# Natural order of the experts, nine tiles before the first expert's rows, and routing groups of 4, 4, 1, 1, 2

## The chip, the cores and the metric

The kernel runs on one core of one Trainium2 chip. The metric is the device time of one execution in microseconds (us), the median of several. Inside the core five engines run side by side, each through its own instructions strictly in their order: TensorE (PE, with its weight loads, PEld), VectorE (DVE), ScalarE (ACT), GpSimd (POOL) and SyncE (SP, which here only starts DMAs). An instruction whose input is not there holds up everything behind it on its engine.

## The reference

Three stages, float32, 1536 tokens of 512 values (2 sequences of 768, 8 heads of 64):

```python
# 1 attention: 4 sink keys and a causal window of 128
keep = is_sink | in_window
a = softmax(where(keep, scores, -1e9));  x = a @ v            # -> (1536, 512)
# 2 mixture of 8 experts, two per token
noisy = x @ w_gate + log1p(exp(x @ w_noise)) * noise          # (1536, 8)
top2  = the two largest of noisy per token; weights = softmax of the two
for e in range(8):
    h = maximum(x[mask] @ w1[e], 0)                           # 512 -> 1024
    out[mask] += weight * (h @ w2[e])                         # 1024 -> 512
# 3 dense layer, 512 -> 2048 -> 512
h = x @ w_in;  out = (h * tanh(softplus(h))) @ w_out
```

## The kernel before

**Stages.** The tokens go through attention in 12 tiles of 128. For each tile the scores of a head are one matmul (line 98), DVE adds the mask and finds the row minimum (line 100), ACT takes the exponential (line 101), PE turns the result (line 108), DVE and ACT copy it from PSUM (lines 110 and 111), and PE multiplies by v (line 120). One step `s` of the loop is half a tile: four heads. Behind it `finish(s,t)` puts the last steps of a tile on later places of the loop: `fin_c` (sinks, copy of x transposed), `fin_d` (gate matmul), `fin_d2` (turns x back, line 171, and scales it, line 173), `fin_d1` (gate values, lines 161 to 165). `SLOW` and `FAST` say how many thirds of a step later each comes.

**Routing.** Tiles are routed in groups. When the last tile of a group is finished, `route` gives nine steps that are placed after it: `absz` (line 187, DVE), `soft` (189 and 190, ACT), `noisy` (192 to 194), `top` (196, 197), `chosen` (199 to 201; the last writes `sl`, the chosen experts as zeros and ones), `place` (on PE the prefix sums over `sl`, lines 208 to 210; on DVE lines 214 to 216, the last writes `slot`, the row of each token in its expert's area), `rest` (231, 232; the counts `cum`, and the scatters), `weights` (235 to 241) and `count` (244, 245). The tiny DVE instructions handle all tiles of a group at once, so their number hardly grows with the group.

**Scatter and load.** POOL then scatters each tile's x into the DRAM buffer `xg` (line 219), two indirect DMAs per tile, one for each chosen expert. Expert areas are 1536 rows apart. As soon as 16 scatters are issued (8 tiles), SP is given the loads of rows 0 to 255 of the first expert (line 817, `load_x(0,0)` and `load_x(0,1)`); they wait until those scatters have landed. This is sound only if the first expert has 256 rows after eight tiles; `ORDER` puts expert 4 first for that, and `flag` (line 338) compares the count and sends the program into `general`, a slow full computation, where it isn't so. In the same way line 339 looks at expert 7 and lines 340 to 344 at the largest and smallest expert.

**Experts.** The loaded rows are turned on PE (`trans_x`, line 575) and split into a high part `xh` (ACT, line 576) and a low part `xl` (DVE, line 577). Every product is three matmuls (high-high, low-high, high-low). The first expert starts on 256 rows only: `l1(0,f,0,256)` for eight column blocks f, 12 matmuls each (line 593), with ACT line 597 and DVE line 600 behind each, and for the first four of them a weight split (ACT line 553, DVE line 557). The routing of the last group (tiles 10 and 11) runs between these blocks: `rq` is a list from which one entry is taken before and one after each `l1`; `GAPS` says how many empty entries follow each step. After the eight blocks come the second layer `l2(0,0)` and `l2(0,1)` (line 621), and in the middle of `l2(0,1)` the remaining rows of the first expert, 256 to 447, are turned (line 575 again). Their loads wait for all 24 scatters. From then on experts 0 to 7 and the dense layer (lines 713 and 738) follow as almost gapless matmul work.

Two lines matter for what follows:

```python
for k in range(n): V.max(v8[:,k,:],nl[:,k,:])                 # 196, one per tile of the group
for k in range(n): V.max_index(i8[:,k,:],v8[:,k,:],nl[:,k,:]) # 197
```

Of the kernel before, what the change touches and what calls it, by code (L numbers as in the profile page):

```python
# [11 lines left out]
F32=mybir.dt.float32; F32R=mybir.dt.float32r; BF=mybir.dt.bfloat16; I32=mybir.dt.int32; U32=mybir.dt.uint32  # L12
# [1 line left out]
PS=bass.MemoryType.PSUM; DR=bass.MemoryType.DRAM  # L14
U32=mybir.dt.uint32
NEG=-1.0e30
GROUPS=(4,4,2,2)
ROWS7=(128,192)
XB=8
GD=(9,11); LGU=3; ZU=8; LSU=(2,30); WB=(2,4,3)  # L20
# [1 line left out]
WLD=0  # L22
NBS=2
EV=((1,),(1,),(1,),(1,),(1,))+((1,3),)*7
LXB=1; XLU=48; BANKS=(('a',6),('c',2)); BN='aa'; RQ=(1,1); GAPS=(1,0,0,0,3,2,3,0,1)

SLOW=(2,5,6,6); FAST={9:(2,3,4,3),10:(2,4,5,6),11:(2,3,4,3)}; FASTR=(0,0,1,2,2,5,5,6,7); SLOWR=(0,0,1,2,3,5,5,6,7)
EXPERT_STRIDE=1536

ORDER=(4,0,1,2,3,5,6,7)  # L30


def attention(ctx, tc, I, st, C=448, LO=256, dbg=None, W=None):

    nc=tc.nc
# [4 lines left out]
    one=pool('a_one',1); ld=pool('a_ld',2); wk=pool('a_wk',WB[0]); w3=pool('a_w3',WB[1]); end=st['end']  # L40
# [14 lines left out]
    noise=end.tile([128,NT,8],F32,name='noise',bufs=1)  # L55
# [5 lines left out]
    for j in range(3):  # L61
        z=bm[32*j:32*j+32]; nc.gpsimd.memset(z,1.0)
# [8 lines left out]
    QD,V,VS,P,NB,RS,XTP,XTS={}, {}, {}, {}, {}, {}, {}, {}  # L71
# [105 lines left out]
    def route(t0,n,one=one):  # L177
# [39 lines left out]
        def scatter(t,k):  # L217
            nc.gpsimd.memset(spacer,0.0)
            d=nc.gpsimd.indirect_dma_start(out=st['xg'],out_offset=bass.IndirectOffsetOnAxis(ap=st['slot'][:,2*t+k:2*t+k+1],axis=0),in_=st['x',t],in_offset=None)
            for e in scat: tc.declare_no_dep(d.ins,e.ins,reason="rows of other tokens")  # L220

            if len(scat)>=16:
                for e in st['early']: tc.declare_no_dep(d.ins,e.ins,reason="rows of other tokens")
            scat.append(d)
        def rest():
# [31 lines left out]
    def at(h,f): fill.setdefault(h,[]).append(f)  # L257
    def slot(h):
        for f in fill.pop(h,()): f()
    def finish(s,t):  # L260

        o=FAST.get(t,SLOW)
        for k,f in zip(o,(fin_c,fin_d,fin_d2,fin_d1)): at(3*s+k,lambda f=f: f(t))
        if t in groups and t<NT-1:
            for k,f in zip(FASTR if t in FAST else SLOWR,route(*groups[t])):
                if f.__name__!='count' or t in (3,7): at(3*s+o[3]+k,f)
    def place_rows(n):
        for _ in range(min(n,len(scq))): scq.pop(0)()

# [1 line left out]
    for s in range(NS+2):  # L271
        t=s//2
        for u in (2*s,2*s+1):
            if s>=NS: break
            p=u%4
            if p==0 and t+2<NT: load(t+2)
            if u>=ZU and (u-ZU)%2==0 and u<ZU+16: st['zero']((u-ZU)//2,zt)
            if u==WLD: W.load_to(W.ahead)
            if u==3: W.scalars()
            if u==LGU:  # L280
                for j in range(2): nc.vector.tensor_copy(wbd[64*j:64*j+64,:,16*j:16*j+16],wg[64*j:64*j+64])
            if u in LSU: load_sinks(LSU.index(u))
# [12 lines left out]
        place_rows(NBS)
        if len(scat)>=16 and W.xload: W.xload(); W.xload=None
    while scq: place_rows(1)
    assert W.xload is None
    st['route']=route; st['scq']=scq; st['rest']=[fill[h] for h in sorted(fill)]
# [2 lines left out]
def host(inp):  # L302
    q,k,v=inp['q'],inp['k'],inp['v']
    B,H,S,D=q.shape
    qT=q.reshape(B,4,2,6,128,D).transpose(0,3,2,5,1,4).reshape(12,2,D,4,128)
    kt=k.reshape(B,4,2,6,128,D).transpose(0,3,2,5,1,4)
    ks=np.broadcast_to(k.reshape(B,4,2,S,D)[:,:,:,:4].transpose(0,2,4,1,3)[:,None],(B,6,2,D,4,4))
    kT=np.concatenate([ks,kt],-1).reshape(12,2,D,4,132)
    R={}
    for n,z in (('q',qT),('k',kT)):  # L310
        R[n+'P']=np.ascontiguousarray(z).reshape(12,128,4,z.shape[-1])
    vv=np.ascontiguousarray(v.transpose(0,2,1,3)).reshape(1536,512)
    wg=np.ascontiguousarray(np.concatenate([inp['moe_w_gate'][:,ORDER],inp['moe_w_noise'][:,ORDER]],1).reshape(4,128,16).transpose(1,0,2))
    return {**R,'v':vv,'wg':wg,'noise':np.ascontiguousarray(inp['moe_noise'][:,ORDER].reshape(12,128,8).transpose(1,0,2))}


def scalars(tc,I,st):
# [8 lines left out]
def flag(tc,st,C,M=256,LO=256):  # L326

    V=tc.nc.vector; f=st['sf']; n=st['cnt']; w=st['sw']; s=f[:,8:15]; i=w[:,4:5]
    v=f[:,0:2]; lo,hi,g=f[:,2:6:2],f[:,3:6:2],f[:,6:8]
    V.tensor_copy(f[:,2:6],w[:,0:4])  # L330
    V.tensor_scalar(g,lo,0.0,4294967296.0,op0=ALU.is_lt,op1=ALU.mult)
    V.scalar_tensor_tensor(v,hi,4294967296.0,lo,op0=ALU.mult,op1=ALU.add)
    V.tensor_tensor(v,v,g,op=ALU.add)

    V.tensor_scalar(s[:,0:1],f[:,0:1],4.0,None,op0=ALU.not_equal)
    V.tensor_scalar(s[:,1:2],f[:,1:2],128.0,None,op0=ALU.not_equal)

    V.tensor_scalar(s[:,2:3],n[:,7,0:1],float(M),None,op0=ALU.is_lt)
    for j,r in enumerate(ROWS7): V.tensor_scalar(s[:,4+j:5+j],n[:,2*j+1,7:8],float(r),None,op0=ALU.is_gt)
    V.tensor_reduce(s[:,3:4],n[:,11,:],axis=AX.X,op=ALU.max)  # L340
    V.tensor_scalar(s[:,3:4],s[:,3:4],float(C),None,op0=ALU.is_gt)

    V.tensor_reduce(s[:,6:7],n[:,11,:],axis=AX.X,op=ALU.min)
    V.tensor_scalar(s[:,6:7],s[:,6:7],float(LO),None,op0=ALU.is_lt)
    V.tensor_reduce(f[:,15:16],s,axis=AX.X,op=ALU.max)
    V.tensor_copy(i,f[:,15:16])
    st['flag']=i

def general(tc,I,st,W32,out):

    nc=tc.nc; ident=st['ident']; NT=12; E=8
    with ExitStack() as ctx:
# [87 lines left out]
        with ExitStack() as ph:  # L440
            a1=pool('g_c1',1,ph)
            nc.vector.memset(X,0.0)
            for e in range(E):
                w1=a1.tile([128,4,1024],F32,name='gw1'); nc.sync.dma_start(w1,I['w1'][ORDER[e]].rearrange("(k p) f -> p k f",p=128))
                w2=a1.tile([128,8,512],F32,name='gw2'); nc.sync.dma_start(w2,I['w2'][ORDER[e]].rearrange("(k p) f -> p k f",p=128))
                hh=a1.tile([128,8,1536],F32,name='ghh')
                for f in range(8):
                    for g in range(3):
# [40 lines left out]
class Weights:  # L489

    def __init__(s, nc, I, W32):
        s.nc=nc; s.src=[]
        for e in range(8):
            w=I['w1']
            for f in range(2): s.src.append(bass.AP(tensor=w.tensor,offset=w.offset+ORDER[e]*512*1024+f*512,ap=[[1024,128],[128*1024,4],[1,512]]))
            w=I['w2']
            for f in range(2): s.src.append(bass.AP(tensor=w.tensor,offset=w.offset+ORDER[e]*1024*512+f*512*512,ap=[[512,128],[128*512,4],[1,512]]))
        w=W32[0]
        for f in range(4): s.src.append(bass.AP(tensor=w.tensor,offset=w.offset+f*512,ap=[[2048,128],[128*2048,4],[1,512]]))
        w=W32[1]  # L500
# [61 lines left out]
def moe(ctx, tc, I, st, W, out, C=448, dbg=None, W32=None):  # L562
# [285 lines left out]
```

## Time and profile before

| | |
|---|---|
| time, median of 3 runs | 725.09 us (724.52 to 725.22) |
| the profiled execution | 723.85 us, of which its span 722.1 us |
| PE busy | 701.2 us, 97% of the span |
| DVE, ACT, POOL busy | 69%, 52%, 48% |
| granted TensorE clock, mean | 0.997 of full speed |

The profile is of one execution; times inside it are counted from the start of its span. The time around the span is 1.75 us, and the median lies 1.24 us above the profiled execution. The attention fills about the first 109 us. PE's busy time is no measure of its speed there, since its pipelined instructions overlap in the record; waits and the order of events say more.

### The profile page before, as it was taken

To read this page: it belongs to the slowest core of one execution; us is meant where nothing else is said; L and a number is where in the kernel's file an instruction comes from. 1 tells how busy PE (TensorE), PEld (TensorE's weight loads), DVE (VectorE), ACT (ScalarE), POOL (GpSimd) and SP (SyncE) were. 2 spreads that over 40 slices of the span, in tenths; PEclk is the share of its full clock that TensorE was granted. 3 is DMA by queue.
4 is the path that set the end of the run, shared out by engine and by line. 5 is a ranking of instruction groups with operands and counts; after the bars stand their busy time and mean duration, and the time that the engine had idled before them with its cause. 6 is when DMAs were issued, how large, how long until landed. Compare 5 with 4: busy or idle time off the path is not lost.

```text
span 722.1 us, 11302 instructions
## 1 busy us (share of the span) xinstructions
PE 701.2 (97%) x3887; PEld 589.3 (82%) x3887; DVE 501.7 (69%) x1107; ACT 376.6 (52%) x835; POOL 344.4 (48%) x313
## 2 busy tenths in 40 slices
PE   6999899999999999999999999999999999999996
PEld 4776679889898888889898888888888888888884
DVE  4788877689698797979876126799955665454441
ACT  4887763455455454545454445466645544453442
POOL 5336462555364544645454474566774343233221
PEclk9999999999999999999999999999999999999998
DMA  8996364588778678778767356322212010010001
GB/s 264 245 267 205 107 227 149 188 267 278 226 233 255 226 243 277 231 256 247 264 203 224 127 175 185 101 89 73 59 30 85 17 30 1 1 58 1 1 0 63
DMA packets 66448, 111.49 MB, mean 154 GB/s; under 512 B 6672, under 2 KB 21264, under 8 KB 66384
## 3 DMA queue, kind: packets, MB, share of 16 engines
q1 hardware_dynamic: 57520, 90.29, 40.0%
q0 software_dynamic: 3840, 12.59, 5.3%
q10 hardware_dynamic: 5024, 7.83, 3.0%
q8 instruction: 32, 0.52, 0.3%
q14 instruction: 32, 0.26, 0.1%
HBM read 82.36 MB, written 28.31 MB: 153 GB/s over the span
## 4 chain that ended last, share of the span: by engine, by line
PE 86%; DVE 5%; DMA 4%; ACT 2%; issue 1%; POOL 1%; SPq 0%; ACTq 0%; DVEq 0%; POOLq 0%
PE a L593 22%; PE o L738 18%; PE h L713 17%; PE c L621 16%; PE c L618 4%; PE a L98 2%; PE c L120 2%; PE a L575 2%; PE a L108 2%; DMA qp<-in_qP_dram 1%; DMA d<-yd,sloty 1%; ACT p L101 1%; DVE tt L100 1%; DMA xg<-xr,slot 1%; DMA vt<-in_v_dram 1%
## 5 line engine op out<-in xcount | busy, mean ns | idle before, releaser
L557 POOL TENSOR_TENSOR wl<-stg,wh 128x512 fp32r<-128x512 f32 x152 | 200.9, 1331 | 166.7 <-ACT wh L553 158.5
L726 POOL TENSOR_TENSOR u<-u,q 128x512 f32<-128x512 f32 x48 | 77.2, 1609 | 138.3 <-DVE u L721 94.8
L553 ACT ACTIVATE wh<-stg 128x512 fp32r<-128x512 f32 x160 | 99.3, 625 | 37.3 <-DMA stg<-in_w_dram 9.8
L593 PE MATMUL a<-xl,wh 128*128 128x448 f32 (+1 forms) x288 | 100.0, 347 | 0.5 <-DVE xl L577 0.5
L593 PE MATMUL a<-xh,wh 128*128 128x448 f32 (+1 forms) x288 | 100.2, 348 | 0.0
L593 PE MATMUL a<-xh,wl 128*128 128x448 f32 (+1 forms) x288 | 99.9, 347 | 0.0
L718 ACT ACTIVATE u<-h 128x512 f32<-128x512 f32 x47 | 28.1, 597 | 119.5 <-PE h L713 98.2
L719 DVE TENSOR_SCALAR u<-u 128x512 f32<-128x512 f32 x48 | 28.0, 583 | 88.5 <-ACT u L718 88.3
L621 PE MATMUL c<-wh,hh 128*128 128x512 f32 x192 | 77.6, 404 | 0.0
L713 PE MATMUL h<-xh,wh 128*128 128x512 f32 (+1 forms) x200 | 76.2, 381 | 0.0
L713 PE MATMUL h<-xl,wh 128*128 128x512 f32 (+1 forms) x200 | 75.4, 377 | 0.2 <-DVE xl L694 0.2
L713 PE MATMUL h<-xh,wl 128*128 128x512 f32 (+1 forms) x200 | 75.3, 377 | 0.0
L738 PE MATMUL o<-wh,gh 128*128 128x512 f32 x192 | 74.8, 390 | 0.4 <-DVE u L721 0.4
L621 PE MATMUL c<-wh,hl 128*128 128x512 f32 x192 | 75.1, 391 | 0.0
L621 PE MATMUL c<-wl,hh 128*128 128x512 f32 x192 | 74.8, 390 | 0.0
L738 PE MATMUL o<-wh,gl 128*128 128x512 f32 x192 | 74.7, 389 | 0.0
L738 PE MATMUL o<-wl,gh 128*128 128x512 f32 x192 | 74.7, 389 | 0.0
L521 DVE TENSOR_SCALAR dh<-dh 128x256 f32<-128x256 f32 x64 | 46.6, 727 | 27.1 <-ACT dh L519 27.0
L597 ACT ACTIVATE hh<-a 128x448 fp32r<-128x448 f32 (+2 forms) x80 | 36.5, 467 | 50.7 <-PE a L593 49.4
L593 PEld LDWEIGHTS a<-xl,wh 128*128 128x128 f32 x288 | 54.3, 189 | 4.2 <-DVE xl L577 0.7
L101 ACT ACTIVATE p<-tt,nb 128x264 f32<-128x264 f32 (+1 forms) x96 | 46.5, 486 | 21.5 <-DVE nb L100 17.0
L593 PEld LDWEIGHTS a<-xh,wh 128*128 128x128 f32 x288 | 54.3, 189 | 3.6
(186 smaller groups left out, 1448.0 us busy)
## 6 DMA issues: line engine op xcount, KB each, us to landing
stg<-in_w_dram SPq DMA_DIRECT2D x64, 512.0 KB, 4.9
d<-in_w_in_dram SPq DMA_DIRECT2D x32, 256.0 KB, 3.6
d<-in_w_out_dram SPq DMA_DIRECT2D x32, 256.0 KB, 3.7
xr<-xg SPq DMA_DIRECT2D x24, 256.0 KB, 4.6
yd<-ys ACTq DMA_DIRECT2D x23, 256.0 KB, 4.2
wi<-dh SPq DMA_DIRECT2D x32, 128.0 KB, 3.7
wo<-dh SPq DMA_DIRECT2D x32, 128.0 KB, 3.4
stg<-wi SPq DMA_DIRECT2D x8, 512.0 KB, 4.3
```

Source lines behind the costliest of these rows:

```text
L101: nc.scalar.activation(o,tt[:,:n],AF.Exp,bias=NB[t][:,h:h+1],scale=-1.0,accum_out=RS[t][:,h:h+1])
L521: h=T[i][1]; nc.vector.tensor_scalar(h,h,lo,hi,op0=ALU.max,op1=ALU.min)
L553: if hi=='act': s.nc.scalar.activation(h,src,AF.Copy)
L557: (s.nc.gpsimd if lo=='pool' else s.nc.vector).tensor_tensor(s.lo[n][:,j,:],s.stg[n,j//2][:,j%2,:],s.hi[n][:,j,:].bitcast(F32),op=ALU.subt ...
L593: nc.tensor.matmul(p[:,:w],a[:,k,fs],b[:,k,c0:c1],start=(i==0),stop=(i==11)); i+=1
L597: for a,b in seg(c0+skip,c1,t): nc.scalar.activation(high(e,f,a,b),p[:,a-c0:b-c0],AF.Relu)
L618: for i,w in enumerate((wh,wl)): nc.tensor.matmul(p[:2*m],HH[f][:,o:o+2*m],w,start=f+i==0,stop=f==7 and i==1)
L621: for i,(h,w) in enumerate(((high(e,f,o,o+m),wh),(high(e,f,o,o+m),wl),(HL[f][:,d:d+m],wh))): nc.tensor.matmul(p[:m],h,w,start=f+i==0,stop= ...
L713: nc.tensor.matmul(p[:,c],a[:,k,fs],b[:,k,c],start=(i==0),stop=(i==11)); i+=1
L718: nc.scalar.activation(u,p,AF.Exp)
L726: nc.gpsimd.tensor_tensor(u,u,q,op=ALU.mult)
L738: nc.tensor.matmul(O[g][i],a[:,s],w[:,k,:],start=(f==0 and j==0),stop=(f==15 and j==2))
```

## The change

The experts keep their natural order (`ORDER` goes, in the gate weights, the noise, the expert weights and the general path). The first expert is now expert 0, and its 256 rows are asked for when nine tiles (18 scatters) are out; `flag` looks at its count after nine tiles (`n[:,8,0]`). For that tile 8 is routed alone and then tile 9 alone, in place of 8 and 9 together, and tile 8's last steps come earlier (`FAST` has an entry for it). The count for the flag is taken at tile 8 in place of tile 7's. The steps of the last routing stand closer in `rq`.

```diff
-GROUPS=(4,4,2,2)
+GROUPS=(4,4,1,1,2)
-LXB=1; XLU=48; BANKS=(('a',6),('c',2)); BN='aa'; RQ=(1,1); GAPS=(1,0,0,0,3,2,3,0,1)
+LXB=1; XLU=48; BANKS=(('a',6),('c',2)); BN='aa'; RQ=(1,1)
-SLOW=(2,5,6,6); FAST={9:(2,3,4,3),10:(2,4,5,6),11:(2,3,4,3)}; ...
+SLOW=(2,5,6,6); FAST={8:(2,4,5,5),9:(2,3,4,3),10:(2,4,5,6),11:(2,3,4,3)}; ...
-ORDER=(4,0,1,2,3,5,6,7)
...
-            if len(scat)>=16:
+            if len(scat)>=18:
                 for e in st['early']: tc.declare_no_dep(d.ins,e.ins,reason="rows of other tokens")
...
-                if f.__name__!='count' or t in (3,7): at(3*s+o[3]+k,f)
+                if f.__name__!='count' or t in (3,8): at(3*s+o[3]+k,f)
...
-        if len(scat)>=16 and W.xload: W.xload(); W.xload=None
+        if len(scat)>=18 and W.xload: W.xload(); W.xload=None
...
-    V.tensor_scalar(s[:,2:3],n[:,7,0:1],float(M),None,op0=ALU.is_lt)
+    V.tensor_scalar(s[:,2:3],n[:,8,0:1],float(M),None,op0=ALU.is_lt)
...
-    rq=[lambda z=z: [f() for f in z] for z in st['rest']]
-    for f,k in zip(st['route'](12-GROUPS[-1],GROUPS[-1],one=st['const']),GAPS): rq+=[f]+[lambda: None]*k
+    z=[lambda z=z: [f() for f in z] for z in st['rest']]; R=st['route'](12-GROUPS[-1],GROUPS[-1],one=st['const']); nop=lambda: None
+    rq=[z[0],R[0],*z[1:],*R[1:5],nop,*R[5:8],nop,R[8]]
```

The line numbers of the changed file are 2 lower than before's in the parts quoted below. On SP and POOL the order of the instructions is the same as before.

DVE, the routing of tiles 8 and 9 in before, from `absz` to `chosen` (`u`, `nl`, `v`, `i`, `eA`, `s`, `sl` are the routing's small tiles, x is tile 9's):

```order
L187 SCALAR_TENSOR_TENSOR u_1612<-lz 128x16
L111 COPY pts<-a 128x512
L173 TENSOR_TENSOR x<-a,recip 128x512
L192 SCALAR_TENSOR_TENSOR nl_1613<-lz,u_1612 128x16
L193 TENSOR_TENSOR nl_1613<-nl_1613,noise 128x16
L194 TENSOR_TENSOR nl_1613<-nl_1613,lz 128x16
L196 MAX v_1614<-nl_1613 128x8 x2
L197 MAX_INDEX i_1615<-v_1614,nl_1613 128x8 x2
L199 TENSOR_TENSOR eA_1616<-i_1615 128x2 x2
L200 TENSOR_TENSOR s_1617<-iota_156,eA_1616 128x32
L201 TENSOR_TENSOR sl_1618<-s_1617 128x16
L123 TENSOR_SCALAR recip<-rs 128x8
```

The same place in the change: tile 9's routing begins (`u_1629`), and the end of tile 8's stands in between.

```order
L185 SCALAR_TENSOR_TENSOR u_1629<-lz 128x8
L109 COPY pts<-a 128x512
L212 TENSOR_TENSOR s_1451<-s_1451,a 128x16
L213 TENSOR_REDUCE sf_1453<-s_1451 128x2
L214 SCALAR_TENSOR_TENSOR slot<-eA_1450,sf_1453 128x2
L226 TENSOR_TENSOR cum<-cum,sl_1452 128x8
L171 TENSOR_TENSOR x<-a,recip 128x512
L190 SCALAR_TENSOR_TENSOR nl_1630<-lz,u_1629 128x8
L191 TENSOR_TENSOR nl_1630<-nl_1630,noise 128x8
L192 TENSOR_TENSOR nl_1630<-nl_1630,lz 128x8
L233 TENSOR_SCALAR sf_1453<-sf_1453 128x2
L234 SCALAR_TENSOR_TENSOR sloty<-eA_1450,sf_1453 128x2
```

Each row now handles one tile, and all of `absz` to `weights` is there twice; tile 8's first half (`absz` to `chosen`) stands one step of the loop earlier on DVE.

ACT, a step earlier, in before: the copy `sk` of tile 9's sinks (line 129), for which DVE's line 130 waits, comes straight after the two small copies.

```order
L110 ACTIVATE pts<-a 128x512
L138 ACTIVATE sc<-p 128x96
L158 ACTIVATE gs<-a 128x128
L129 ACTIVATE sk<-a 96x128
L101 ACTIVATE p,rs<-tt,nb 128x264 x4
```

In the change:

```order
L108 ACTIVATE pts<-a 128x512
L156 ACTIVATE gs<-a 128x128
L136 ACTIVATE sc<-p 128x96
L187 ACTIVATE u_1446<-u_1446 128x8
L188 ACTIVATE u_1446<-u_1446 128x8
L127 ACTIVATE sk<-a 96x128
L99 ACTIVATE p,rs<-tt,nb 128x264 x4
```

Tile 8's `soft` (two rows) stands ahead of `sk`; and on DVE tile 8's x, gate values and `absz` stand ahead of the instruction that waits for `sk`.

PE, the prefix sums of the last routing among the blocks `l1(0,f)` in before: `wl_745` is a weight tile of blocks 4 to 7, and the sums come between blocks 5 and 6.

```order
L593 MATMUL a<-xh,wl_745 128x256
L208 LDWEIGHTS tri
L208 MATMUL a<-sl_1882,tri 128x8
L210 LDWEIGHTS ones
L210 MATMUL a<-cum,ones 128x8
```

In the change (`wl_467` is a weight tile of blocks 0 to 3):

```order
L591 MATMUL a<-xh,wl_467 128x256
L206 LDWEIGHTS tri
L206 MATMUL a<-sl_1906,tri 128x8
L208 LDWEIGHTS ones
L208 MATMUL a<-cum,ones 128x8
```

The sums moved up by two blocks, to between blocks 3 and 4. On DVE the rows ahead of the last `sl` are the same as before but for one: line 600 of block 3 now stands behind it.

## Rows read from the trace of the kernel before

**Rows 1.** The page, the chain that ended last, shares of the span by engine.

```profile
PE 86%; DVE 5%; DMA 4%; ACT 2%; issue 1%; POOL 1%; SPq 0%; ACTq 0%; DVEq 0%; POOLq 0%
```

**Rows 2.** Stretches: length, busy us of PE, PEld, DVE, ACT, POOL, granted clock, DMA.

```profile
80.00:103.50 23.50, 21.41 (x228) 16.75 (x227) 22.02 (x114) 16.67 (x58) 9.37 (x18) 1.00 0.37 136
103.50:109.00 5.50, 5.50 (x67) 4.82 (x59) 2.65 (x9) 2.43 (x7) 3.19 (x7) 1.00 0.73 281
109.00:132.00 23.00, 20.89 (x143) 18.90 (x143) 14.77 (x62) 7.54 (x18) 6.69 (x9) 1.00 0.42 145
```

**Rows 3.** Waits from 80 to 109 us: us in total, times, longest.

```profile
ACT p L101 <- DVE nb L100: 6.7, 5, 2.2
DVE tt L100 <- PE a L98: 0.4, 1, 0.4
```

**Rows 4.** Timeline of DVE: start, us, operation; routing of tiles 8 and 9.

```profile
95.76 0.17 DVE L187 SCALAR_TENSOR_TENSOR u<-lz 128x16 f32<-128x16 f32 x1
95.86 0.68 DVE L111 COPY pts<-a 128x512 f32<-128x512 f32 x1
...
97.06 0.16 DVE L192 SCALAR_TENSOR_TENSOR nl<-lz,u 128x16 f32<-128x16 f32 x1
...
98.87 0.17 DVE L123 TENSOR_SCALAR recip<-rs 128x8 f32<-128x8 f32 x1
...
101.64 0.17 DVE L214 TENSOR_TENSOR s<-s,a 128x32 f32<-128x32 f32 x1
...
102.84 0.68 DVE L111 COPY pts<-a 128x512 f32<-128x512 f32 x1
```

**Rows 5.** Timeline of DVE and ACT, `absz` with `soft`, and the sinks' copy.

```profile
82.71 0.19 DVE L187 SCALAR_TENSOR_TENSOR u<-lz 128x32 f32<-128x32 f32 x1
...
83.33 0.58 ACT L110 ACTIVATE pts<-a 128x512 f32<-128x512 f32 x1
...
88.58 0.16 DVE L123 TENSOR_SCALAR recip<-rs 128x8 f32<-128x8 f32 x1
88.58 0.27 ACT L129 ACTIVATE sk<-a 96x128 fp32r<-96x128 f32 x1 [0.24 <-PE a L126]
...
88.89 0.29 DVE L130 TENSOR_TENSOR sk<-a,sk 32x128 fp32r<-32x128 f32 x1
```

**Rows 6.** Timeline, scatters 15 and 16, the first two loads, their first use.

```profile
96.24 0.96 POOL L219 DMA_INDIRECT xg<-x,slot  x1 [0.21 <-issue]
...
97.51 0.96 POOL L219 DMA_INDIRECT xg<-x,slot  x1 [0.23 <-issue]
...
100.30 1.10 SPq L817 DMA_DIRECT2D xr<-xg  x2
...
106.93 1.06 PE L575 MATMUL a<-ident,xr 128*128 128x128 f32 x8
```

**Rows 7.** Line 817 over the whole run, from issue to landing.

```profile
DMA to landing us min/median/max: 4.5/5.3/7.1
```

**Rows 8.** Timeline of the last routing, from block 4 to the remaining rows' turning.

```profile
115.81 0.28 PE L593 MATMUL a<-xh,wh 128*128 128x256 f32 x1
117.73 0.17 DVE L201 TENSOR_TENSOR sl<-s 128x16 bf16<-128x16 f32 x1
118.70 0.18 PE L208 MATMUL a<-sl,tri 128*128 128x8 bf16 x1
120.08 0.16 DVE L216 SCALAR_TENSOR_TENSOR slot<-eA,sf 128x4 int32<-128x4 f32 x1
120.52 0.96 POOL L219 DMA_INDIRECT xg<-xr,slot  x1 [13.18 <-DVE slot L216]
128.81 0.89 SPq L817 DMA_DIRECT2D xr<-xg  x2
131.85 1.05 PE L575 MATMUL a<-ident,xr 128*128 128x128 f32 x8 [1.61 <-DMA xr<-xg]
```

More of the change, by code (lines that the diff above doesn't have):

```diff
@@ L24 @@
 EV=((1,),(1,),(1,),(1,),(1,))+((1,3),)*7
-LXB=1; XLU=48; BANKS=(('a',6),('c',2)); BN='aa'; RQ=(1,1); GAPS=(1,0,0,0,3,2,3,0,1)
-SLOW=(2,5,6,6); FAST={9:(2,3,4,3),10:(2,4,5,6),11:(2,3,4,3)}; FASTR=(0,0,1,2,2,5,5,6,7); SLOWR=(0,0,1,2,3,5,5,6,7)
+LXB=1; XLU=48; BANKS=(('a',6),('c',2)); BN='aa'; RQ=(1,1)
+SLOW=(2,5,6,6); FAST={8:(2,4,5,5),9:(2,3,4,3),10:(2,4,5,6),11:(2,3,4,3)}; FASTR=(0,0,1,2,2,5,5,6,7); SLOWR=(0,0,1,2,3,5,5,6,7)
 EXPERT_STRIDE=1536
-ORDER=(4,0,1,2,3,5,6,7)
 def attention(ctx, tc, I, st, C=448, LO=256, dbg=None, W=None):
@@ L312, in host @@
     vv=np.ascontiguousarray(v.transpose(0,2,1,3)).reshape(1536,512)
-    wg=np.ascontiguousarray(np.concatenate([inp['moe_w_gate'][:,ORDER],inp['moe_w_noise'][:,ORDER]],1).reshape(4,128,16).transpose(1,0,2))
-    return {**R,'v':vv,'wg':wg,'noise':np.ascontiguousarray(inp['moe_noise'][:,ORDER].reshape(12,128,8).transpose(1,0,2))}
+    wg=np.ascontiguousarray(np.concatenate([inp['moe_w_gate'],inp['moe_w_noise']],1).reshape(4,128,16).transpose(1,0,2))
+    return {**R,'v':vv,'wg':wg,'noise':np.ascontiguousarray(inp['moe_noise'].reshape(12,128,8).transpose(1,0,2))}
 def scalars(tc,I,st):
@@ L443, in general @@
             for e in range(E):
-                w1=a1.tile([128,4,1024],F32,name='gw1'); nc.sync.dma_start(w1,I['w1'][ORDER[e]].rearrange("(k p) f -> p k f",p=128))
-                w2=a1.tile([128,8,512],F32,name='gw2'); nc.sync.dma_start(w2,I['w2'][ORDER[e]].rearrange("(k p) f -> p k f",p=128))
+                w1=a1.tile([128,4,1024],F32,name='gw1'); nc.sync.dma_start(w1,I['w1'][e].rearrange("(k p) f -> p k f",p=128))
+                w2=a1.tile([128,8,512],F32,name='gw2'); nc.sync.dma_start(w2,I['w2'][e].rearrange("(k p) f -> p k f",p=128))
                 hh=a1.tile([128,8,1536],F32,name='ghh')
@@ L494, in __init__ @@
             w=I['w1']
-            for f in range(2): s.src.append(bass.AP(tensor=w.tensor,offset=w.offset+ORDER[e]*512*1024+f*512,ap=[[1024,128],[128*1024,4],[1,512]]))
+            for f in range(2): s.src.append(bass.AP(tensor=w.tensor,offset=w.offset+e*512*1024+f*512,ap=[[1024,128],[128*1024,4],[1,512]]))
             w=I['w2']
-            for f in range(2): s.src.append(bass.AP(tensor=w.tensor,offset=w.offset+ORDER[e]*1024*512+f*512*512,ap=[[512,128],[128*512,4],[1,512]]))
+            for f in range(2): s.src.append(bass.AP(tensor=w.tensor,offset=w.offset+e*1024*512+f*512*512,ap=[[512,128],[128*512,4],[1,512]]))
         w=W32[0]
```

## The prediction, made before the changed kernel ran

> **What bounds the kernel now.** I read the chain that ended last, then the stretches between 80 and 132 us, then the waits and the timeline there, because the change moves instructions only there. The chain is 86% PE [rows 1], and behind 132 us that means matmuls without gaps. The chain alone doesn't say what sets the end of the attention. The stretches do: from 80 to 103.5 us DVE is busy 22.02 of 23.5 us, PE 21.41, but PE's times overlap in the record [rows 2]. Who waits for whom decides: ACT waited 6.7 us in five waits for DVE's row minima (line 100), while DVE waited for PE's scores once, 0.4 us [rows 3]. So up to 103.5 us DVE is the clock, and what is added to it ahead of the last scores comes out at the end of the attention. From 103.5 to 109 us DVE is busy 2.65 of 5.5 us; there PE works off the last tiles, in order. From 109 us on PE is the clock, with one wait that matters: at 131.85 us it has waited 1.61 us for the remaining rows of the first expert [rows 8].
>
> **The second routing on DVE.** In before tiles 8 and 9 cost DVE one set of small instructions: 0.10 us for `absz` (95.76 to 95.86), 1.81 for `noisy` to `chosen` (97.06 to 98.87), 1.20 for `place` to `weights` (101.64 to 102.84), together 3.11 us for 23 instructions [rows 4] (a `max_index` is two). A group of one tile has 19: one MAX, two of the index, and one of `rest` fall away. By their number that is 3.11 x 19/23 = 2.57 us; if only the instruction of `rest` saves anything, 3.11 x 22/23 = 2.97. I take 2.8, between the two, because most of these instructions need the one ahead and so don't get closer in a smaller group. The first half, `absz` to `chosen`, is 1.91 us for 14 instructions; with 11 it is 1.50 to 1.91, and I take 1.75. Ahead of the last four score instructions DVE had one first half (1.91); now it has all of tile 8 (2.8) and the first half of tile 9 (1.75). That is 2.64 us more, between 2.57 + 1.50 - 1.91 = 2.16 and 2.97. The rest of tile 9 comes behind the last scores, where before had more. Tile 8's x and gate values are moved, not added.
>
> [...]
>
> **A wait of DVE for the sinks.** Tile 8's `absz` now stands on DVE directly ahead of tile 9's `recip` (line 123) and `sk` (line 130), and on ACT `soft` stands ahead of the copy for which line 130 waits. From `absz` to the end of `soft` are 0.62 us (82.71 to 83.33) and from the copy to line 130 another 0.31 (88.58 to 88.89) [rows 5]: 0.93 us, in which DVE has work for 0.10 + 0.17. That is an idle 0.66, of which before has 0.31 - 0.17 = 0.14. So +0.5; nothing, if DVE comes there late for other reasons. Queued behind it are the next four score instructions, for which ACT waits. In return DVE's one wait for scores, 0.4 us [rows 3], goes, since DVE is now later than PE there.
>
> **End of the attention:** 2.6 + 0.5 - 0.4 = 2.7 us later, bounds 2.16 - 0.4 = 1.8 and 2.97 + 0.5 = 3.5. PE comes to the turning of the first expert's rows at 106.93 + 2.7 = 109.6 us.
>
> **The first rows, after 18 scatters.** In before the sixteenth was issued at 97.51, SP's loads started 2.79 us later, at 100.30, and PE used them at 106.93 without a wait [rows 6]. Now DVE comes to the copy that stood at 95.86 [rows 4] by 1.75 + 0.5 - 0.4 later, at 97.7; with the copy (0.7) and two small instructions (0.4) tile 8's `slot` begins at 98.8, and the scatter 0.44 after it (120.08 to 120.52, [rows 8]) at 99.2, when POOL is just free of the sixteenth. Scatters follow each other by 1.27 us (96.24 to 97.51), so the eighteenth goes at 100.5, has landed at 103.3, and the loads land 5.3 us later, at 108.6 and half of 1.10 after that [rows 6, 7]. PE comes at 109.6 and needs the second half a turning later, at 110.1. I cost it at nothing; the attention's own 2.7 us hide it. Should a load take the 7.1 us of the slowest, the second is there at 110.95 and PE waits 0.8. What stands behind these loads on SP (a stage of weights, line 545) starts 3 us later; the four weight splits of the blocks that follow use stages loaded before.
>
> **The last routing.** The sums (line 208) now stand two blocks earlier on PE: it asks for `sl` when block 3 is done, in before's times at 115.81, where before asked at 118.70. But in before `sl` began on DVE only at 117.73 and was there at 117.9 [rows 8]. Ahead of it DVE has the same instructions as before but one, line 600 of block 3, and ACT's `soft` now delays one weight split by about as much; I keep 117.9, give or take 0.4. So PE waits 117.9 - 115.8 = 2.1 us, and blocks 4 to 7 and the second layer stand behind it. It reaches the remaining rows 2.1 us later than its 131.85 - 1.61 = 130.24, at 132.3. They are there at 131.85 or earlier, so the 1.61 us go, and 0.5 is lost (all of this 2.7 later). Were there no wait for `sl`, this part would give 1.6 back; with 2.5 us it costs 0.9.
>
> **The rest costs nothing.** The order of the experts changes only addresses. The count for the flag is one small copy (line 245) and one sum in either. SP and POOL have the same order.
>
> **Sum:** 2.7 + 0.5 = 3.2 us. The profiled execution of 723.85 us would be 727.05; the median lies 1.24 above it, so **728.3 us**. Its own bounds: 1.8 + 0.1 (`sl` 0.4 earlier) and 3.5 + 0.9, that is 727.0 to 729.5. The runs of before spread over 0.7 us; 0.2%, 1.45 us, is about what a measurement can tell from no change.
>
> **Rivals.**
> - *No wait for `sl`* (0.14): ACT and DVE catch up, `sl` is there when block 3 ends, and the 1.61 us come back: 2.7 - 1.6 = +1.1, 726.2 us. It takes DVE 2.1 us earlier than in before; DVE was busy only 14.77 of 23 us there [rows 2], but the instructions ahead of `sl` are tied to the blocks' ends.
> - *The rows come late* (0.10): DMA slower than [rows 7], or `slot` later; each us beyond the 0.5 of cover counts in full. With 0.8 to 1.5: 729 to 730.
> - *Cheap small instructions* (0.06): they follow each other by 0.10 as `absz` and its neighbour do [rows 4]; 30 x 0.10 - 1.91 = 1.1 in place of 2.6, so 1.7 in all, 726.8 us. The mean of 3.11/23 = 0.135 speaks against it. [...]
> - *DVE has room* (0.07), the other sign: its idle 1.5 us before 103.5 and 2.85 after it [rows 2] take up all that is added, neither the last scores nor `sl` come late, and the 1.61 us are gained: 725.1 - 1.6 = 723.5 us. It decides for "faster" only if what DVE costs, both places together, stays under 0.16 us. ACT's 6.7 us of waiting for DVE speak against it.
> [...]
> - *The change doesn't do what it says* (0.01): with fewer than 256 rows for expert 0 after nine tiles the general path would run as well, far outside any range given here. Counted from the reference with its seed 0 there are 287 (252 after eight).
>
> **How the numbers follow.** My forecast has 0.60. The range goes from just under the first rival to the late rows, 726.0 to 730.0; it holds forecast, first three rivals, without their tails. Faster: the fourth rival, 0.07. Same (up to 726.54): the first rival and a little of the third, 0.16. Slower: 0.77.
>
> **What would show it.** Right: between 86 and 104 us DVE still without gaps but for one before line 130; the last four score instructions some 2.7 us later; no wait at the first turning; a wait of about 2 us at line 208 (206 in the changed file) in the blocks, and none at the second turning. Wrong: DVE waiting for PE's scores more than once, a wait of PE for `xr` at the first turning, or `sl` ahead of PE.

## The result and the profile after

| | before | changed |
|---|---|---|
| median of 10 runs | 723.29 us (722.00 to 725.24) | 727.46 us (726.21 to 730.25) |
| ratio | | 1.0058 [1.0043, 1.0073] |
| profiled execution, its span | 723.85, 722.1 | 728.75, 726.6 |
| mean granted clock of that execution | 0.997 | 0.990 |

The changed kernel is 4.2 us slower. These runs and those of the first four experiments met a kernel before of 723.2 to 723.3 us ("the first chips" below), the eight kernels after them ran on two other chips where it takes 737.8 and 739.3 us, so each kernel is compared only with runs of before on its own chip.

The chain that ended last, shares by engine, to be held against [rows 1]: PE as before, DVE and ACT one more each, DMA one less.

```profile
PE 86%; DVE 6%; DMA 3%; ACT 3%; issue 1%; POOL 1%; SPq 0%; ACTq 0%; DVEq 0%; POOLq 0%
```

Waits between 80 and 111 us (in total, times, longest), to be held against [rows 3]:

```profile
ACT p L99 <- DVE nb L98: 8.1, 5, 2.9
PE a L106 <- DVE sk L128: 1.8, 2, 1.3
DVE sk L128 <- ACT sk L127: 0.6, 1, 0.6
```

ACT waits more for DVE's row minima (8.1 in place of 6.7 us). DVE no longer waits for scores, and has the new wait of 0.6 for the sinks' copy. In no term of the prediction: PE waits for DVE's `sk`, 1.3 us at the longest, where before had 0.2.

DVE's timeline, to be held against [rows 4, 5]: the sinks' wait, tile 8's `slot`, tile 9's `absz` and `sl`, the last four score instructions.

```profile
90.56 0.29 DVE L128 TENSOR_TENSOR sk<-a,sk 32x128 fp32r<-32x128 f32 x1 [0.60 <-ACT sk L127]
...
97.26 0.22 DVE L185 SCALAR_TENSOR_TENSOR u<-lz 128x8 f32<-128x8 f32 x1
...
98.40 0.16 DVE L214 SCALAR_TENSOR_TENSOR slot<-eA,sf 128x2 int32<-128x2 f32 x1
...
100.99 0.17 DVE L199 TENSOR_TENSOR sl<-s 128x8 bf16<-128x8 f32 x1
...
101.82 0.43 DVE L98 CUSTOM_DVE_ANT_0 tt<-a,m 128x264 f32<-128x264 f32 x1
```

PE's timeline, to be held against [rows 6, 8]: PE's wait for `sk`, the first turning, the sums of the last routing, the second turning.

```profile
101.61 1.93 PE L106 MATMUL a<-ident,p 128*128 128x128 f32 x8 [1.35 <-DVE sk L128]
103.47 1.88 PE L118 MATMUL c<-pts,vt 128*64 128x128 f32 x16
...
110.52 1.06 PE L573 MATMUL a<-ident,xr 128*128 128x128 f32 x8
...
121.25 0.18 PE L206 MATMUL a<-sl,tri 128*128 128x8 bf16 x1 [1.70 <-DVE sl L199]
...
137.03 0.99 PE L573 MATMUL a<-ident,xr 128*128 128x128 f32 x8
```

Both turnings come without a wait. The wait for `sl` is where the prediction put it. But behind both waits PE is slow: line 118's 16 matmuls take 1.88 us, where the same 16 of before (line 120) took 1.09:

```profile
99.99 1.09 PE L120 MATMUL c<-pts,vt 128*64 128x128 f32 x16
```

The stretches (columns as in [rows 2]; the granted clock stands third from the right) say why:

```profile
88.40:101.60 13.20, 10.44 (x93) 7.86 (x92) 11.79 (x65) 6.99 (x26) 10.47 (x20) 1.00 0.47 180
101.60:105.30 3.70, 3.69 (x25) 3.10 (x26) 2.36 (x11) 2.58 (x9) 0.00 (x0) 0.54 0.60 181
105.30:110.50 5.20, 5.20 (x66) 4.32 (x65) 3.21 (x14) 1.81 (x5) 2.10 (x4) 1.00 0.69 227
110.50:121.20 10.70, 8.55 (x70) 8.11 (x69) 7.53 (x28) 5.51 (x13) 0.00 (x0) 1.00 0.13 27
121.20:126.00 4.80, 4.75 (x31) 4.71 (x32) 2.65 (x12) 0.38 (x1) 2.64 (x5) 0.64 0.76 281
```

Right behind each of PE's two new waits the mean granted clock was 0.54 and 0.64; in steps of 0.1 us it stood at 0.50 from 101.7 to 105.1 us, where most of line 118's 16 matmuls lie, and from 122.2 to 125.5. In the other three stretches the mean was 1.00. In before it was at 1.00 there throughout [rows 2].

The first rows' way went as forecast: tile 8's second scatter and the loads' issue (line 817 of before), to be held against [rows 6]:

```profile
100.09 0.96 POOL L217 DMA_INDIRECT xg<-x,slot  x1 [0.23 <-issue]
...
102.84 1.10 SPq L816 DMA_DIRECT2D xr<-xg  x2
```

### The profile page after: what moved, and what is told of

It reads as the page before. It is cut to its first block, busy times and chain, and to the rows that moved or that the text cites. A ratio compares the mean times of both kernels' runs of the same rounds, so it can differ in the third digit from the quotient of the medians.

```text
span 726.6 us, 11322 instructions
## 1 busy us (share of the span) xinstructions
PE 703.8 (97%) x3886; PEld 591.6 (81%) x3886; DVE 503.4 (69%) x1122; ACT 376.1 (52%) x837; POOL 343.9 (47%) x313
## 4 chain that ended last, share of the span: by engine, by line
PE 86%; DVE 6%; DMA 3%; ACT 3%; issue 1%; POOL 1%; SPq 0%; ACTq 0%; DVEq 0%; POOLq 0%
PE a L591 22%; PE o L737 18%; PE h L712 17%; PE c L619 17%; PE c L616 4%; PE c L118 2%; PE a L573 2%; PE a L96 2%; PE a L106 2%; DMA qp<-in_qP_dram 1%; ACT p L99 1%; DVE tt L98 1%; DMA stg<-wi 1%; DMA vt<-in_v_dram 1%; PE xt L690 0%
## 5 line engine op out<-in xcount | busy, mean ns | idle before, releaser
L519 DVE TENSOR_SCALAR dh<-dh 128x256 f32<-128x256 f32 x64 | 48.9, 763 | 27.2 <-ACT dh L517 27.2
L99 ACT ACTIVATE p<-tt,nb 128x264 f32<-128x264 f32 (+1 forms) x96 | 46.5, 486 | 22.5 <-DVE nb L98 18.4
```

What stands on the lines that cost most here:

```text
L99: nc.scalar.activation(o,tt[:,:n],AF.Exp,bias=NB[t][:,h:h+1],scale=-1.0,accum_out=RS[t][:,h:h+1])
L519: h=T[i][1]; nc.vector.tensor_scalar(h,h,lo,hi,op0=ALU.max,op1=ALU.min)
```

## The experiments

**Theory:** the attention ends some 2.4 us later because of the second routing on DVE; in the last routing a wait for `sl` takes the place of the one at the second turning, at about the same price; and PE's new waits let the clock fall, which costs more. **Rivals:** the low clock is an accident of one execution; or the last routing's order is the main cost.

A common zero is needed, since all starts differ by up to 1 us: DVE's sum of the counts of tiles 4 to 7 (`cum<-cum,cw`, 88.49 in before, 88.27 in after). Times behind it, read from the timelines of PE and DVE on the first chips (the last of the four score instructions starts 1.06 us behind the first, at 12.19 and 14.61):

| us behind the zero | before | changed, 1st | changed, 2nd | old order | spare matmuls | split on POOL |
|---|---|---|---|---|---|---|
| first of the last four score instructions | 11.13 | 13.55 | 13.54 | 13.54 | 13.54 | 13.55 |
| first turning | 18.44 | 22.25 | 20.90 | 20.90 | 21.18 | 20.91 |
| second turning | 43.36 | 48.76 | 45.91 | 45.55 | 47.00 | 48.32 |
| from first to second | 24.92 | 26.51 | 25.01 | 24.65 | 25.82 | 27.41 |

The new order of the experts, which no run changes by itself, costs nothing behind the table: from the second turning to the end of the span are 590.25 us in before (722.1 less 131.85) and 589.57 in the changed kernel (726.6 less 137.03).

**1. The changed kernel once more**, no edit.

> The changed kernel once more, beside the others on one chip. Theory (what its trace showed): against before the last scores on DVE come 2.2 us later because of the second routing; PE waits 1.35 us for DVE's sinks (line 128) and 1.70 us for sl (line 206), and after each of the two waits the granted clock is at half for some 3.5 us, which costs about 1.4 and 1.5 us; the 1.61 us wait at the second turning is gone. So again 4 us over before, and both stretches at the low clock in the trace. Rival: the low clock is an accident of that one profile; then one or both stretches are at 1.00 here and the time is 2 to 3 us over before.

Measured: 727.87 us, 1.0061 [1.0046, 1.0077]. Both waits stand in its profile (1.35 and 1.69 us), yet the stretches behind them are at full clock:

```profile
101.10:105.00 3.90, 3.85 (x42) 3.11 (x46) 3.59 (x20) 3.07 (x10) 0.55 (x1) 1.00 0.54 168
...
119.30:126.00 6.70, 6.67 (x57) 6.54 (x58) 3.33 (x15) 1.53 (x5) 4.09 (x7) 1.00 0.85 312
```

So the waits stand in both executions, the clock's fall in one of them. The table prices it: without it 2.46 us more than before at the first turning and 2.55 at the second; with it 3.81 and 5.40, so the two low stretches cost about 1.35 and 1.5.

This execution lost 1.2 us elsewhere. Behind the fourth turning of rows PE waits for the last low half of the next expert's rows:

```profile
161.53 0.47 PE L591 MATMUL a<-xl,wh 128*128 128x448 f32 x1 [1.19 <-DVE xl L575]
```

The same wait, 0.9 to 1.3 us, stands in six of the 14 profiles of this study, one of them of before itself (below). It isn't tied to the change; an execution has it or not.

**2. The waits filled:** 9 spare matmuls ahead of the wait for `sk`, 12 ahead of the sums.

```diff
             ps=misc()
+            if t0==10:
+                for _ in range(12): nc.tensor.matmul(ps[:,128:256],ident,ident,start=True,stop=True)
...
             c=misc(); nc.tensor.matmul(c[:,0:8],ones,cum,start=True,stop=True)
+            if t0==8:
+                for _ in range(9): nc.tensor.matmul(c[:,128:256],ident,ident,start=True,stop=True)
```

> The changed kernel with spare matmuls (identity by identity, into unused columns of PSUM tiles that PE holds anyway) queued just before its two waits: 9 behind the count at tile 8, 12 ahead of the last routing's sums. They add work that lies in the waits. Theory (waiting PE loses its clock, and that costs 2.9 us): the granted clock stays at 1.00 from 100 to 130 us, PE reaches the second turning about 2.9 us earlier than in the changed kernel, and the time is 1.3 to 2 us over before. Rival (the clock falls for another reason, or the low clock hides in waits that would come anyway): same time as the changed kernel, or slower by the 2.9 us that the spare matmuls take.

Measured: 728.49 us, 1.0066 [1.0052, 1.0079]: 5.3 us above before, not the 1.3 to 2 expected. The matmuls took longer than the waits (2.25 and 2.84 us), which costs 1.1 up to the second turning by the table. No stretch from 88 to 135 us is below 1.00:

```profile
101.70:105.30 3.60, 3.60 (x42) 3.26 (x41) 3.01 (x17) 2.71 (x10) 0.00 (x0) 1.00 0.51 146
...
121.20:126.00 4.80, 4.80 (x46) 4.75 (x45) 2.15 (x13) 0.77 (x2) 3.15 (x6) 1.00 0.78 266
```

Its five runs spread over 1.5 us (727.91 to 729.37) and have mean clocks of 0.996 to 0.999, where the changed kernel's first ten spread over 4.0 at 0.990 to 0.999. That alone proves little: the changed kernel's six runs of experiment 1, on the same chip, have mean clocks of 0.995 to 0.999 too and spread over 3.2 us, and its profile had no fall either. Less the 1.1 the median would be 727.4, an estimate: by it the clock costs the changed kernel's median on this chip (727.87) about half a microsecond, not three, and that is within the spread of the runs.

**3. The old order of the last routing** in the changed kernel.

```diff
-    rq=[z[0],R[0],*z[1:],*R[1:5],nop,*R[5:8],nop,R[8]]
+    rq=[*z]
+    for f,k in zip(R,(1,0,0,0,3,2,3,0,1)): rq+=[f]+[nop]*k
```

> The changed kernel with the last routing's steps as far apart as in before (its sums between blocks 5 and 6). Theory: no wait of PE for sl, no low clock behind it (1.85 + 1.5 us less), and the wait of 1.6 us at the second turning is back: 1.7 us faster than the changed kernel, 2.4 over before. Rival (following closely pays, the wait for the rows is worth more): slower than the changed kernel by up to 1.6 us.

Measured: 727.0 us, 1.0048 [1.0031, 1.0064]. No wait for `sl`; the wait at the second turning is back:

```profile
PE a L573 <- DMA xr<-xg: 1.7, 2, 1.3
```

Against experiment 1 it gains 0.36 us up to the second turning, and 0.9 in the medians, whose intervals overlap; expected were 1.7, with the cost of the clock counted in. So most of the loss, 3.8 of 4.7 us on this chip, comes with groups and experts' order, and little with the last routing's order.

**4. `sl` sooner?** DVE's four weight splits in the blocks go to POOL, to take 0.68 us each out of DVE's way to `sl`.

```diff
-        if W.k<16: W.split(lo='dve')
+        if W.k<16: W.split(lo='pool')
```

> The changed kernel with the low halves of the four weight splits among the blocks on POOL in place of DVE (line 555, 0.6 us of DVE each; POOL is idle there). Theory: sl comes about 1.8 to 2.4 us earlier, when block 3 ends; PE doesn't wait for it (less than 0.4 us), the clock behind it stays at 1.00, and the 1.61 us at the second turning stay away: 3 us faster than the changed kernel, 0.5 to 1.5 over before. Rival (sl is tied to the blocks' ends by ACT and line 598, not to DVE's load): the wait stays over 1.3 us and the time is that of the changed kernel.

Measured: 727.99 us, 1.0064 [1.0043, 1.0086], and `sl` came later; PE waited 2.6 in place of 1.7. DVE's and then POOL's timeline:

```profile
117.49 1.15 DVE L197 TENSOR_TENSOR eA<-i 128x2 f32<-128x2 uint32 x2
118.68 1.18 DVE L198 TENSOR_TENSOR s<-iota,eA 128x32 f32<-128x32 f32 x1
119.89 0.17 DVE L199 TENSOR_TENSOR sl<-s 128x16 bf16<-128x16 f32 x1
...
116.03 3.78 POOL L555 TENSOR_TENSOR wl<-stg,wh 128x512 fp32r<-128x512 f32 x3 [0.92 <-ACT wh L551]
```

The first two rows (the first is two instructions) take 1.15 and 1.18 us in place of the 0.23 and 0.19 of experiment 1, and end about when POOL's second and third of the three splits do; MAX and the index beside them kept their times (0.23 and 0.16 us). Why these two took longer and those not is not shown.

In its profile the clock did fall behind the wait for `sl`; that is 1.5 of the 2.4 us by which the turnings lie further apart than in experiment 1 (27.41 against 25.01), and the longer wait is 0.9:

```profile
120.00:124.50 4.50, 4.38 (x28) 4.38 (x29) 2.03 (x12) 0.38 (x1) 2.74 (x5) 0.62 0.98 348
```

**The later eight kernels** met something that the first chips don't show. The kernel before, profiled there with no edit:

> The kernel before, profiled once more. The profiled execution of the changed kernel's second run lost 1.2 us at about 160 us, where PE waited for DVE's low half of the next expert's rows, and two of the four changed kernels show this wait, but neither the first profile of before nor the first of after. If this wait is a matter of chance in every kernel, the times of before in the second profile agree with the first up to the second turning (last scores 12.2 us, first turning 18.4, second turning 43.4 us behind the sum of tiles 4 to 7 on DVE, each within 0.3), and the wait may stand here too. If it comes from the change, it is absent here. No low clock between 90 and 140 us by the theory that the two new waits of PE are what lets it fall; if it falls here too, the clock has nothing to do with the change.

It took 739.21 us (one run; median of before there 737.81). Its timelines of ACT, DVE and POOL:

```profile
99.99 0.60 ACT L147 ACTIVATE xts<-c 128x512 f32<-128x512 f32 x1 [6.58 <-remote]
...
117.18 0.27 ACT L129 ACTIVATE sk<-a 96x128 fp32r<-96x128 f32 x1 [4.27 <-remote]
...
100.14 0.43 DVE L100 CUSTOM_DVE_ANT_0 tt<-a,m 128x264 f32<-128x264 f32 x1 [6.98 <-remote]
...
97.35 0.96 POOL L219 DMA_INDIRECT xg<-x,slot  x1 [0.22 <-issue]
...
115.17 0.96 POOL L219 DMA_INDIRECT xg<-x,slot  x1 [0.21 <-issue]
```

ACT and DVE stand twice, for nothing that the profile can name ("remote"), PE with them. They go on 2.6 us behind tile 7's last scatter (97.35) and 2.0 behind tile 9's (115.17); the eight scatters between 80 and 100 us in before on the first chip landed 2.8 us after their issue (median). In before on the first chip ACT's line 147 stood at 92.87 with a wait of 0.36. So the agreement within 0.3 us that was expected is missed: the first turning comes 30.5 us behind the zero, not 18.4. Behind each stand the clock is near 0.5 (stretches):

```profile
100.00:104.00 4.00, 3.36 (x16) 3.36 (x17) 2.84 (x12) 3.12 (x11) 0.00 (x0) 0.50 0.55 187
...
112.00:116.00 4.00, 3.25 (x46) 2.47 (x46) 0.40 (x1) 0.92 (x3) 3.34 (x7) 1.00 0.49 188
116.00:120.00 4.00, 1.71 (x15) 1.68 (x16) 1.93 (x6) 1.27 (x4) 0.21 (x2) 1.00 0.19 74
120.00:124.00 4.00, 4.00 (x19) 3.70 (x19) 1.86 (x4) 0.57 (x2) 0.00 (x0) 0.52 0.02 6
```

The low clock is thus there without the change too, but again behind places where PE stood. And the 1.2 us wait of experiment 1 is there too, in before:

```profile
PE a L593 <- DVE xl L577: 1.3, 1, 1.3
```

**5. Only the last routing's new order**, in the kernel before; run on both chips.

```diff
-    rq=[lambda z=z: [f() for f in z] for z in st['rest']]
-    for f,k in zip(st['route'](12-GROUPS[-1],GROUPS[-1],one=st['const']),GAPS): rq+=[f]+[lambda: None]*k
+    z=[lambda z=z: [f() for f in z] for z in st['rest']]; R=st['route'](12-GROUPS[-1],GROUPS[-1],one=st['const']); nop=lambda: None
+    rq=[z[0],R[0],*z[1:],*R[1:5],nop,*R[5:8],nop,R[8]]
```

> The kernel before with the last routing's steps of the changed kernel, and nothing else. By the reasons as the runs so far leave them: PE waits 1.7 to 2.1 us for sl in the blocks and no longer at the second turning, which comes 0.1 to 0.5 us later than before; 0 to +0.5 us, 723.2 to 723.7, and up to 1.5 more in executions in which the clock falls after the wait. By the rival that this order gives back the second turning's 1.61 us because sl is early when DVE has no second routing ahead of it: 1.6 less, 721.6. By the rival that this order carries most of the change's 4 us: 726 or more.

> The kernel before with the last routing's steps of the changed kernel, once more: in the first run of it the kernel before itself took 737.8 us, because ACT, DVE and PE stood for 4 to 7 us twice between 93 and 117 us, waiting for nothing that the profile names. Without these stands the two explanations are as before: PE waits 1.7 to 2.1 us for sl in the blocks and not at the second turning, 0 to +0.5 us against before, up to 1.5 more where the clock falls; or sl is early and 1.6 us are gained; or the order carries most of the 4 us. Where the stands are there again, they move sl and the rows alike and the difference is again within 1.5 us.

Measured: 0.9984 [0.9965, 1.0003] and 0.9988 [0.9968, 1.0009]. PE waits 1.7 us for `sl` and not at the second turning (waits of the second run):

```profile
PE c L145 <- DVE sk L130: 3.2, 1, 3.2
PE a L208 <- DVE sl L201: 1.7, 1, 1.7
```

That this order carries most of the 4 us is out. Between no difference and a gain of 1.6 us the intervals don't decide; the wait for `sl` is there also without a second routing ahead of it.

**6. Spare matmuls of the right number**, 5 and 7, in the changed kernel; run on both chips.

```diff
+                for _ in range(7): nc.tensor.matmul(ps[:,128:256],ident,ident,start=True,stop=True)
...
+                for _ in range(5): nc.tensor.matmul(c[:,128:256],ident,ident,start=True,stop=True)
```

> The changed kernel with 5 spare matmuls of ident by ident behind the count of tile 8 and 7 ahead of the last routing's sums, by the 0.24 us each that the longer lists of the earlier run took: 1.25 and 1.66 us, as long as the waits that they stand in. They fill PE's waits and add nothing behind them. If the half clock after the waits is caused by PE standing idle, no stretch between 96 and 139 us is below 1.00 and the runs lie 1.5 to 2 us below those with 9 and 12 spare matmuls, that is at 726.5 to 727, at or up to 1 us below the changed kernel, with less spread than its 3 us. If the clock falls whatever PE does, low stretches are there too, and the median is the changed kernel's or above.

> The changed kernel with 5 and 7 spare matmuls in PE's two new waits, once more, for the same reason. By the theory that PE's standing idle lets the clock fall: no stretch below 1.00 between 96 and 139 us, 2.9 to 3.7 us above before, where the changed kernel was 4.2 to 4.6 above it. By the theory that the clock falls whatever PE does: low stretches there, and 4 us or more above before. With the stands of the other run present, below before, as there (1.8 us).

Measured: 0.9976 [0.9955, 0.9998] and 0.9926 [0.9900, 0.9951]: on these chips *faster* than before, by 1.8 and 5.5 us. The first expectation had been written for the first chip and fails by the sign. The first stand is there, with a clock of 0.50 behind it, the second isn't: the four scatters of tiles 8 and 9 now go in two pairs that start 7.3 us apart, and ACT and DVE have no "remote" wait behind 102 us. Behind 108 us the clock is 1.00, as the theory of PE's standing idle has it. The same stretches as above, of the second run:

```profile
112.00:116.00 4.00, 4.00 (x50) 3.26 (x50) 1.68 (x9) 1.81 (x5) 2.10 (x4) 1.00 0.85 295
116.00:120.00 4.00, 3.56 (x37) 3.08 (x33) 2.85 (x8) 1.85 (x4) 0.00 (x0) 1.00 0.24 92
120.00:124.00 4.00, 3.59 (x30) 3.59 (x31) 2.42 (x7) 1.01 (x3) 0.00 (x0) 1.00 0.00 0
```

How the changed kernel fares there without spare matmuls was not run.

**7. Tiles 8 and 9 as one group**, natural order and 18 scatters kept; run on both chips.

```diff
-GROUPS=(4,4,1,1,2)
+GROUPS=(4,4,2,2)
...
-                if f.__name__!='count' or t in (3,8): at(3*s+o[3]+k,f)
+                if f.__name__!='count' or t in (3,9): at(3*s+o[3]+k,f)
...
-    V.tensor_scalar(s[:,2:3],n[:,8,0:1],float(M),None,op0=ALU.is_lt)
+    V.tensor_scalar(s[:,2:3],n[:,9,0:1],float(M),None,op0=ALU.is_lt)
```

> The changed kernel with tiles 8 and 9 routed as one group again (4,4,2,2), still with the rows of the first expert asked for after 18 scatters. DVE has one first half ahead of the last scores as in before, so these should come 12.2 to 12.8 us behind the sum of tiles 4 to 7, 2 us earlier than in the changed kernel, if its second routing on DVE is the cost that I put it down to; 14.6 as in the changed kernel, if that cost lies elsewhere (order of the experts, the count). The 17th and 18th scatter go at about 102.5 and 103.8 us, the loads 2.8 later and land 5.3 behind, at about 112, so PE waits 4 to 5 us at the first turning, and 1.7 for sl in the blocks: the second turning some 5 us later than before, 728 to 728.5, no better than the changed kernel, and worse by 1 to 3 if the clock falls after these waits. By the rival that the loads have several us of room, no wait at the first turning and 725 to 726.

> The changed kernel with tiles 8 and 9 routed as one group, once more, since in its first run the kernel before took 737.8 us. Last scores 12.2 to 12.8 us behind the sum of tiles 4 to 7 if the second routing on DVE is the cost, 14.6 if not. Loads of the first rows land at about 112 us: PE waits 4 to 5 us at the first turning and 1.7 for sl, 4.5 to 5.5 us above before, and 1 to 3 more where the clock falls. By the rival that the loads have several us of room, 1 to 2 us above before.

Measured: 1.0019 [0.9999, 1.0040] and 1.0020 [0.9993, 1.0047]. The question of DVE's cost got no answer: the stand fixes when DVE goes on, and the first of the last four scores starts 18.6 us behind the zero (20.0 in before there). The rows kept PE 0.6 and 0.9 us, not 4 to 5: the second stand is back with four scatters in a row, and in it PE waited 3.2 and 2.4 us ahead of the turning. The waits of the second run:

```profile
PE c L143 <- DVE sk L128: 2.4, 1, 2.4
PE a L206 <- DVE sl L199: 1.7, 1, 1.7
PE a L573 <- DMA xr<-xg: 0.9, 1, 0.9
```

**8. The sums one block earlier than in before**, one later than in the changed kernel.

```diff
-GAPS=(1,0,0,0,3,2,3,0,1)
+GAPS=(1,0,0,0,1,2,3,0,1)
```

> The kernel before with the last routing's sums one block earlier than it has them, one block later than in the changed kernel. By the arithmetic of the prediction: PE asks for sl at 117.25 (block 4's end), DVE has it at 117.9, so 0.65 us of wait; slot and the rows come 0.8 earlier than in before, 131.05, PE comes at 130.24 + 0.65 = 130.89: 0.16 of wait is left of 1.61. In all 0.8 us less than before, a ratio of 0.9989. If sl follows PE's blocks (DVE later whenever PE asks earlier), the wait for sl is 1.2 or more and nothing is gained. If the rows' way after the sums is longer than in before, the second turning still waits 0.5 or more.

Measured: 0.9963 [0.9939, 0.9987]. The waits are what the arithmetic gives, 0.5 us for `sl` (0.65 forecast) and none at the second turning:

```profile
PE c L145 <- DVE xr L173: 1.5, 1, 1.5
PE a L208 <- DVE sl L201: 0.5, 1, 0.5
```

The gain of 2.7 us by the ratio is more than the 0.8 foretold, whose ratio of 0.9989 lies just outside the interval. What made the rest isn't shown; in its profile the second stand is shorter as well, and the instructions up to there are those of before. Against the profile of before on the other late chip the first turning, ahead of which the edit changes nothing, is already 1.6 us early (28.84 against 30.46 us behind the zero), and the second 2.2. It beats before on that chip; on the first chips it wasn't run.

**The clock over all 14 profiles.** Seven have a wait of 1.7 us or more for `sl` ahead of the last routing's sums: both of the changed kernel, the splits on POOL, and experiments 5 and 7 on both chips. In six of them the clock is 0.50 from 2 to 4 us behind the start of the sums; only experiment 1 stays at 1.00. In the other seven PE doesn't wait there, waits 0.5 us, or the wait is filled, and the clock is 1.00 in all. Experiments 5, 7 and 8 in their second or only runs:

```profile
136.00:140.00 4.00, 4.00 (x26) 3.91 (x25) 1.39 (x9) 0.38 (x1) 3.26 (x7) 0.69 0.97 369
...
132.00:136.00 4.00, 4.00 (x27) 3.95 (x27) 1.55 (x9) 0.77 (x2) 3.34 (x7) 0.73 0.96 328
...
132.00:136.00 4.00, 4.00 (x30) 3.71 (x30) 1.97 (x10) 1.01 (x4) 3.35 (x7) 1.00 0.93 348
```

Experiment 5 puts the wait into the kernel before, experiments 2, 3 and 6 take it out of the changed kernel, and the fall comes and goes with it. So the wait for `sl` lets the clock fall to 0.50, in six of the seven profiles that have it. Behind the wait for `sk` it fell in one of the four profiles of the first chips that have this wait unfilled.

## Why the prediction was right, and where it was not

The forecast rested on four terms and a base. The terms can be checked one by one in the traces; no run that changes only DVE's second routing gave an answer (experiment 7), so its cost is read from the rows, not isolated.

**DVE's second routing** (2.64 forecast, bounds 2.16 to 2.97): right in kind, 0.3 too large. In after's timeline tile 8's set is 2.61 us (0.11 + 0.47 + 1.06 + 0.55 + 0.42, five pieces between other work; 2.8 forecast) and tile 9's first half 1.64 (1.75 forecast). Less 1.91 that is 2.34. The small instructions follow each other as in before, about 0.14 us apart, so the rival of cheap small instructions is out.

**The sinks' wait** (0.66 forecast): 0.60. **DVE's wait for scores** (0.4): gone. In sum 2.34 + 0.46 - 0.36 = 2.44, and the last scores came 2.42 later (13.55 against 11.13). That DVE has room is refuted with it.

**The first rows** (hidden): right. `slot` at 98.40 (98.8 forecast), the loads' issue at 102.84 (103.3), no wait at the first turning. The prediction's list of rivals speaks of 0.5 us of cover; its own times leave 1.0 (109.6 against 108.6).

**The last routing** (a wait of 2.1 for `sl`, 0.5 lost): the wait is 1.7, so 1.70 - 1.61 = 0.1 is lost; 25.01 against 24.92 us between the turnings in the execution without low clock.

**What was not in the sum.** PE's wait of 1.35 us for `sk`. It alone delays nothing: at full clock the first turning is 2.46 later, as the last scores are. But it is one of the two waits behind which the clock fell to 0.50. **The granted clock** is in no term of the sum either. Behind the wait for `sl` it falls in six of seven profiles. The price is 1.5 us there, since it lasts about 3.4 us, and 1.35 more where it falls behind the wait for `sk` as well. In another execution of the same kernel it stayed at 1.00 behind both (experiment 1), so a chance that is an on-or-off for the kernel is the wrong form for it.

**0.4 us lie outside the span**, which the prediction left at before's value without a word. The time around the span is 1.71 us in before and 2.13 in the changed kernel (medians over their runs). It is 2.1 to 2.2 in each kernel with five groups but the one with splits on POOL (1.75). Why isn't settled.

**The sum.** 2.5 to 2.6 us in the span at full clock and 0.4 around it are 3.0, near the 3.2 forecast. Measured are 4.2 and 4.7. How the remaining 1.2 to 1.7 divide between the clock and chance waits like that of 1.2 us stays open. For the clock speak the 1.5 us behind the wait for `sl` in most profiles, and the first ten runs: the four with a mean clock of at most 0.992 have a median of 729.4 us, the other six 726.9. Against it speak the six runs of experiment 1, all at 0.995 or more and yet at 727.87, and the half microsecond of experiment 2. A pair of profiles can't settle it, since single executions lie up to 3 us apart: the one of before was 0.6 us above its median of ten, the one of experiment 1 the fastest of its six, 1.1 below their median. The forecast of 728.3 lies only 0.8 above the measured median because a second miss goes the other way, and that is luck: its base, the median of three runs of before (725.09), was 1.8 above that of ten.

## What to carry to other kernels

A new wait can cost more than its length: the wait of 1.7 to 2.6 us for `sl` was followed by a granted clock of 0.50 in six of seven profiles, which cost 1.5 us more in the changed kernel's first. Look at what PE does behind a new wait, and look in more than one execution. Weigh a regrouping of small instructions by their spacing in the trace, times their number, and by what they stand in front of; that sum came out within 0.3 us here. And measure on more than one chip: the same groups cost 4 us on one and, with PE's waits filled, gained 2 to 5 on two others, where the second stand is gone. That the scatters' going in pairs is what removed it is likely but not shown, since the spare matmuls came with it.

## What the runs showed of the hardware

- Behind PE's waits of 1.35 and 1.7 us the granted clock was at 0.50 for about 3.4 us each in one profiled execution and stayed at 1.00 in another of the same kernel. Behind waits of 1.7 to 2.6 us at the last routing's sums it fell to 0.50 in six of seven profiles, and in none of the seven without such a wait there.
- On two chips ACT, DVE and PE stood for 1.5 to 7.4 us while POOL issued four or eight scatters in a row. DVE went on 2.7 to 2.9 us behind the last of the eight; behind the last of the four ACT went on after 2.0 us, but in the profile of experiment 8 after 0.5. On the first chips none of the profiles has it. What they waited for isn't settled.
- A 128x32 instruction on DVE (`s<-iota,eA`) took 1.18 us in place of 0.19 while POOL worked on the low halves of 128x512 weight tiles (1.26 us each).
